# A transformer block on one core: the second MLP weight prepared earlier in parts that share tiles with the transposed rows, sums copied out by ScalarE, rows of x loaded earlier, the norm split by groups

## The chip, the cores and the metric

One Trainium2 chip, one of its NeuronCores. The metric is the device time of the whole program in microseconds (us), the median over runs. Besides, one execution was recorded by the hardware profiler; its span is the time from the first to the last recorded instruction. TensorE (PE) multiplies, VectorE (DVE), ScalarE (ACT) and GpSimd (POOL) work element by element, SyncE (SP) issues nearly all DMA transfers, in one queue.

## The reference

```python
mod = (_silu(c) @ w_mod).reshape(c.shape[0], 6, 1, -1)
sa, ca, ga, sb, cb, gb = (mod[:, i] for i in range(6))
h = _layernorm(x, axis=-1) * (1 + ca) + sa
x = x + ga * _A_ref(h, A_wq, A_wk, A_wv, A_wo)      # 32 query heads of 16, one key/value head
h = _layernorm(x, axis=-1) * (1 + cb) + sb
x = x + gb * _B_ref(h, B_w1, B_b1, B_w2, B_b2)      # gelu(h @ w1 + b1) @ w2 + b2, tanh form
```

x has 2048 rows of 512, all in float32; w1 is 512 x 1376, w2 1376 x 512. A product of full precision is made of three products of rounded parts, high and low: names in H and L are these pairs (`w2H`, `w2L`, `gH`, `gL`, `onH`, `onL`).

## The kernel before

**Blocks, units, steps, cycles.** The 2048 rows are worked off in 8 blocks of 256. Attention of a block is 8 units (`u`, four heads each), a unit is 8 steps over the keys. Two steps make one turn of the main loop, a cycle; `clock[0]` rises by 4 in it. In a cycle TensorE makes 8 products `m` (scores whose row maxima VectorE takes ahead, line 523), 8 products `e` (scores for the exponentials that ScalarE makes, line 599) and at the end of each step 16 products `acc` (line 610, probabilities by values).

**The rest of a block rides along.** Everything after attention, the output product (`wops`), the second layer norm, the transposes (`tp`), the two MLP products (`w1ps`, `w2ps`), is a generator, `rest_steps`, and so are the query projections (`qps`) of later rows. Each cycle takes one batch of products from the first generator that is ready. A batch of more than 4.8 in units of 512 columns (12 products of 256 columns are 6.0) is mixed in as two halves of the rows of the systolic array with one pattern, a lighter one (`LIGHT`) with another pattern that opens with an exponential's product, a cycle without a batch with a third. `W2_PARTS` cuts the 33 products of each of a block's four second MLP sums (two tiles of rows, t, by two halves of the columns) into batches. The fourth sum is put between the next block's `wops` and its transposes (`second`).

**Banks.** Batches' sums lie in one PSUM bank, "x"; it must be read out before the next sum begins. The exponentials' products use three banks in turn. So the element-wise operation that reads a finished sum is waited for by the next sum's first product. `store` does this for the second MLP: VectorE adds the sum to the rows of x (`x1`, tile "x1", two buffers) into `ot`, and SP sends `ot` two clock ticks later.

**Work put off.** `later(n, fn)` runs `fn` n clock ticks on, that is, puts its instructions into the engines' orders there. No scheduler moves anything: the order in which the code runs is the order of each engine, and engines wait for each other by semaphores only. So an engine may run ahead, but SP and GpSimd take their own instructions strictly one after the other.

**From attention to the output product.** When a block's attention ends, `rest` lets SP load the sums (`rsum`), VectorE invert them, SP write them to `drs`, and `fetch_half` load per group g of 128 columns the heads (`os`, from `do`) and the inverted sums (`os`, from `drs`), groups 0 and 1 first, 2 and 3 four ticks later. `norm` then lets GpSimd multiply the four groups and split all of them at once into `onH` and `onL`. `fetch_rest` loads x (512 KB) when the block's output product begins, and three tiles of w1.

**Weights.** Between the attention products GpSimd prepares w1, then wo, then w2, one tile of 128 rows each four ticks (`PREP`): SP loads it (`w2f`, three buffers; the last tile has 96 rows, and GpSimd clears it first), GpSimd multiplies by the gate and splits it. `w2H` and `w2L` are one tile each for all 11 row tiles and take the place of `bigH`, `bigL`, the transposed rows of blocks 1 to 3 (of 512 rows each) that the query projections read. So w2 starts only when the last projection has been sent (`state["q"] == 0`).

**Loads that TensorE must not meet late.** `load_q` loads a unit's queries into `qst`, in six DMAs, two cycles ahead of their first use. `heed` notes each DMA with a tick, and `wait_early` makes an `acc` product that comes after this tick wait for it:

```python
heed(nc.sync.dma_start(out=raw(qst[64 * s:64 * s + 16]), in_=low), n)       # n = 6 if s else 8
...
if kt % 2 or cidx:
    wait_early(ins)                                                          # one DMA per acc product
```

Of the kernel before, what the change touches and what calls it, by code (L numbers as in the profile page):

```python
# [34 lines left out]
LIGHT = 4.8  # L35
Q_LIGHT = 12
Q_SIZES = ((6, 6), (4, 4, 4))
W2_PARTS = ((12, 12, 9), (9, 8, 8, 8), (9, 8, 8, 8), (12, 12, 9))
TAIL = (4, 8)
GROUP = 4  # L40
NORM_WAIT = 8
# [11 lines left out]
def adaln_mqa_mlp(  # L53
# [15 lines left out]
    nc = tc.nc  # L69
    _, S, D = x.shape  # L70
# [3 lines left out]
    KD = D // P  # L74
    BQ = 512
    NB = S // BQ
# [4 lines left out]
    NF = (F + P - 1) // P  # L81
# [4 lines left out]
    blocks = [(r, HQ) for r in range(0, S, HQ)]  # L86

    xf = x[0]
# [3 lines left out]
    att = ctx.enter_context(tc.tile_pool(name="att", bufs=1))  # L92
# [37 lines left out]
    def split(dst_h, dst_l, src, eng_h, eng_l, between=None):  # L130
        if eng_h is nc.gpsimd:
            eng_h.tensor_scalar(out=dst_h, in0=src, scalar1=1.0, scalar2=0.0, op0=ALU.mult, op1=ALU.add)
        elif eng_h is nc.scalar:
            eng_h.copy(dst_h, src)
        else:
            eng_h.tensor_copy(out=dst_h, in_=src)
        if between:
            between()
        eng_l.tensor_tensor(out=dst_l, in0=src, in1=raw(dst_h), op=ALU.subtract)  # L139
# [3 lines left out]
    state = {"mods": False, "q": NB * KD}  # L143
# [193 lines left out]
    hts = {}  # L337
    hts_stats = {}
    pad(att, 64, "pad5")
    bigH = att.tile([P, NB - 1, KD, BQ], F32R, name="bigH", tag="bigH")  # L340
    bigL = att.tile([P, NB - 1, KD, BQ], F32R, name="bigL", tag="bigL")
    hts[0] = (att.tile([P, KD, BQ], F32R, name="h0H", tag="opk"), att.tile([P, KD, BQ], F32R, name="h0L", tag="woH"))
    for b in range(1, NB):
        hts[b] = (bigH[:, b - 1], bigL[:, b - 1])

    pad(att, 64, "pad6")
    tps = {}
# [348 lines left out]
    def rest(b, fast):  # L696

        rp = wts_pool["rest"]
        row0, w = blocks[b]
        spread = ["m", "e", "m", "e", "m", "e", "v"] if fast else ["x"]  # L700
        turn = [0]

        def bank():
            turn[0] += 1
            tag = spread[turn[0] % len(spread)]
            return ebank() if tag == "e" else dict(tag=tag, bufs=3 if tag == "m" else 1)

        oss, ons = {}, {}

        def fetch():  # L710

            n = H * w // P
            rsum = att.tile([P, n], F32, name=f"rsum{b}", tag="rsum", bufs=1)
            nc.sync.dma_start(out=rsum, in_=do[b][:, :, 16, :].rearrange("q c (t n) -> (q c) t n", n=n))

            def invert():
                nc.vector.reciprocal(out=rsum, in_=rsum)
                later(1, scatter)

            def scatter():  # L720
                nc.sync.dma_start(out=drs[b].rearrange("h (t n) -> (h t) n", n=n), in_=rsum)
                fetch_half(0)

            later(4, invert)

        def fetch_half(hf):
            os_ = att.tile([P, 2, KD, HQ], F32, name=f"os{b}_{hf}", tag="opk", bufs=1)
            cols = slice(hf * HQ, (hf + 1) * HQ)

            def fetch_heads(gs):  # L730
                for g in gs:
                    src = do[b][2 * g:2 * g + 2, :, 0:16, cols].rearrange("q c r n -> (q c) r n")
                    nc.sync.dma_start(out=os_[:, 0, g, :], in_=src)
                    src = drs[b][8 * g:8 * g + 8, cols].unsqueeze(1).to_broadcast([8, 16, HQ])
                    nc.sync.dma_start(out=os_[:, 1, g, :], in_=src)


            fetch_heads(range(KD // 2))
            later(4, lambda: fetch_heads(range(KD // 2, KD)))
            oss[hf] = os_  # L740
            later(7, lambda: norm(hf))

        def norm(hf):
            if fast:
                g = KD - 1
                split(state["on"][0][:, g, :], state["on"][1][:, g, :], state["os"][:, 0, g, :], nc.scalar, nc.vector)
                return
            onH = att.tile([P, KD, HQ], F32R, name=f"onH{b}_{hf}", tag="xH", bufs=2)
            onL = att.tile([P, KD, HQ], F32R, name=f"onL{b}_{hf}", tag="xL", bufs=2)
            ons[hf] = (onH, onL)  # L750
            os_ = oss.pop(hf)
            for g in range(KD):
                nc.gpsimd.tensor_tensor(out=os_[:, 0, g, :], in0=os_[:, 0, g, :], in1=os_[:, 1, g, :], op=ALU.mult)  # L753
            split(onH, onL, os_[:, 0], nc.gpsimd, nc.gpsimd)
            if (hf + 1) * HQ < w:
                later(6, lambda: fetch_half(hf + 1))
            ready[hf] = clock[0] + NORM_WAIT

        ready = {}
        later(*((4, lambda: norm(0)) if fast else (2, fetch)))  # L760
        return rest_steps(b, fast, rp, bank, ons, ready)

    early = {}

    def fetch_w1(b, w1ts, f):
        w1ts[f] = wts_pool["rest"].tile([P, 2, KD, P], F32R, name=f"w1t{b}_{f}", tag="w1t", bufs=3)
        heed(nc.sync.dma_start(out=raw(w1ts[f]), in_=dw1[f]), 8 if f > 2 else 24)

    def fetch_rest(b):

        row0, w = blocks[b]
        x1 = wts_pool["rest"].tile([P, 2, D], F32, name=f"x1_{b}", tag="x1", bufs=2)
        nc.sync.dma_start(out=x1, in_=xf[row0:row0 + w, :].rearrange("(t p) d -> p t d", p=P))
        w1ts = {}
        for f in range(3):
            if b == len(blocks) - 1:
                fetch_w1(b, w1ts, f)
            else:
                later(W1_TURNS * (f + 1), lambda f=f: fetch_w1(b, w1ts, f))
        early[b] = x1, w1ts  # L780
# [8 lines left out]
    def rest_steps(b, fast, rp, bank, ons, ready):  # L789
# [6 lines left out]
        for hf in range(w // HQ):  # L796
# [188 lines left out]
            def store(t, ps, cols=slice(0, D)):  # L985
                row = row0 + hf * HQ + t * P
                ot = rp.tile([P, D], F32, name=f"ot{b}_{hf}_{t}_{cols.start}", tag="ot", bufs=2)
                nc.vector.tensor_tensor(out=ot[:, cols], in0=ps[:, :cols.stop - cols.start], in1=x1[:, t, cols], op=ALU.add)  # L988
                send = lambda: nc.sync.dma_start(out=of[row:row + P, cols], in_=ot[:, cols])
                if fast:  # L990
                    send()
                else:
                    later(2, send)
# [4 lines left out]
            def second_sum(t, cols, size):  # L998
                n = cols.stop - cols.start
                sl = slice(t * P, (t + 1) * P)  # L1000
                place = dict(tag="m", bufs=3) if b == len(blocks) - 2 and t else bank()
                ps = psum.tile([P, n], F32, name=f"w2ps{b}_{hf}_{t}_{cols.start}", **place)
                ops = [(gH[:, f, sl], gL[:, f, sl], w2H[:, f, cols], w2L[:, f, cols]) for f in range(NF)]
                yield from batches(ps, ops, size, lambda f: made.issuperset(range(f + 1)))
                if fast:
                    later(1, lambda t=t, ps=ps, cols=cols: store(t, ps, cols))
                    yield 2
                else:
                    store(t, ps, cols)
# [12 lines left out]
    def put_by(b):  # L1022

        return b < len(blocks) - 2
# [90 lines left out]
    def prep_w2():  # L1115
        rp = wts_pool["rest"]
        wfs = {}

        def load(f):
            fw = min(P, F - f * P)  # L1120
            wf = wfs[f] = rp.tile([P, D], F32, name=f"w2f{f}", tag="wf", bufs=3)
            if fw < P:
                nc.gpsimd.memset(wf, 0.0)
            nc.sync.dma_start(out=wf[:fw], in_=w2[f * P:f * P + fw, :])

        def work(f):
            nc.gpsimd.tensor_tensor(out=wfs[f], in0=wfs[f], in1=gb, op=ALU.mult)
            split(w2H[:, f, :], w2L[:, f, :], wfs[f], nc.gpsimd, nc.gpsimd)

        return prepare(NF, load, work)  # L1130

    weights = ["w1", "wo", "w2"]
    preps = {}
# [171 lines left out]
    while mp.done < lead[0]:  # L1305
        chunk(1)
    preps["w1"] = prep_w1()
    w2H = w2L = None
    prepared = [0]

    def issue(*groups):
# [28 lines left out]
    for u in range(NU):  # L1340
        for K in range(0, steps[u], 2):
# [76 lines left out]
            end_step(u, X)  # L1418
            behind = (u, Y)
            clock[0] += 1  # L1420
            if state["mods"] and state["q"] == 0 and w2H is None:
                w2H = att.tile([P, NF, D], F32R, name="w2H", tag="bigH")
                w2L = att.tile([P, NF, D], F32R, name="w2L", tag="bigL")
                preps["w2"] = prep_w2()
            if clock[0] >= prepared[0] + PREP and weights and weights[0] in preps:
                prepared[0] = clock[0]
# [53 lines left out]
```

## Time and profile before

| | us |
|---|---|
| median of 3 runs (1595.82 to 1596.21) | 1595.88 |
| the profiled execution, its own time | 1594.15 |
| its span | 1592.4 |
| TensorE busy in it | 1558.2 |
| VectorE, ScalarE, GpSimd busy in it | 1413.8, 1199.7, 665.5 |

The page's rows name an instruction by engine, source line, operation and tiles, written tile first. TensorE is busy nearly all the time, so the reading turns on the few places where it is not, and on how long each step takes. In a timeline a row is start, length, engine, line, operation, tiles and how many equal instructions were merged; in brackets stands the idle time of the engine before it and what ended it. Times count from the span's start.

### The profile page before, as it was taken

To read this page: it belongs to the slowest core of one execution; us is meant where nothing else is said; L and a number is where in the kernel's file an instruction comes from. 1 tells how busy PE (TensorE), PEld (TensorE's weight loads), DVE (VectorE), ACT (ScalarE), POOL (GpSimd) and SP (SyncE) were. 2 spreads that over 40 slices of the span, in tenths; PEclk is the share of its full clock that TensorE was granted. 3 is DMA by queue.
4 is the path that set the end of the run, shared out by engine and by line. 5 is a ranking of instruction groups with operands and counts; after the bars stand their busy time and mean duration, and the time that the engine had idled before them with its cause. 6 is when DMAs were issued, how large, how long until landed. Compare 5 with 4: busy or idle time off the path is not lost.

```text
span 1592.4 us, 43322 instructions
## 1 busy us (share of the span) xinstructions
PE 1558.2 (98%) x17491; PEld 1044.7 (66%) x17491; DVE 1413.8 (89%) x2515; ACT 1199.7 (75%) x2393; POOL 665.5 (42%) x1176
## 2 busy tenths in 40 slices
PE   6999999899999999999999999999999999999999
PEld 3466655557666676666767676666766676666767
DVE  7899999799999999999999999999999999999715
ACT  5577777678877887778877887778877788778853
POOL 4445431686503372235612364224712364224721
PEclk8999999999999999999999999999999999999999
DMA  8136311413112120212112130212112130121231
GB/s 264 70 112 204 113 55 58 129 40 108 33 53 69 47 95 22 89 35 90 51 37 87 44 99 19 64 59 83 57 35 88 35 109 19 48 82 52 96 135 72
DMA packets 81022, 121.74 MB, mean 76 GB/s; under 512 B 15966, under 2 KB 55646, under 8 KB 80564
## 3 DMA queue, kind: packets, MB, share of 16 engines
q1 hardware_dynamic: 80804, 118.95, 22.9%
q8 instruction: 137, 2.24, 0.6%
q14 instruction: 65, 0.53, 0.1%
q10 hardware_dynamic: 16, 0.00, 0.0%
HBM read 91.13 MB, written 27.27 MB: 74 GB/s over the span
## 4 chain that ended last, share of the span: by engine, by line
PE 86%; DVE 6%; POOL 3%; DMA 2%; SPq 1%; issue 1%; ACT 0%; DVEq 0%; POOLq 0%; ACTq 0%
PE acc L610 29%; PE e L598 17%; PE m L518 17%; PE w1ps L193 8%; PE w2ps L193 6%; DVE mx L523 5%; PE wops L193 3%; PE qps L193 2%; PE w2ps L187 2%; PE w1ps L187 1%; DMA xt<-in_A_x_dram 1%; PE tp L193 1%; PE kps L164 1%; DMA os<-drs 1%; DMA x<-in_A_x_dram 0%
## 5 line engine op out<-in xcount | busy, mean ns | idle before, releaser
L523 DVE TENSOR_REDUCE mx<-m 128x1 f32<-128x512 f32 x2048 | 1272.6, 680 | 97.4 <-PE m L518 83.6
L599 ACT ACTIVATE p<-e 128x512 f32<-128x512 f32 x2048 | 1065.5, 601 | 307.5 <-PE e L598 212.4
L518 PE MATMUL m<-ks,qst 64*128 64x512 f32 x2048 | 829.7, 434 | 7.2 <-DMA qst<-dq 4.0
L598 PE MATMUL e<-qst,ks 64*128 64x512 f32 x2048 | 737.5, 412 | 1.4 <-ACT wqH L334 1.3
L610 PE MATMUL acc<-p,va 128*32 128x256 f32 x8192 | 549.6, 386 | 0.0
L598 PEld LDWEIGHTS e<-qst,ks 64*128 64x128 f32 x2048 | 361.1, 185 | 113.4 <-ACT p L599 103.9
L518 PEld LDWEIGHTS m<-ks,qst 64*128 64x128 f32 x2048 | 367.8, 184 | 101.9 <-DVE mx L523 81.7
L610 PEld LDWEIGHTS acc<-p,va 128*32 128x32 f32 x8192 | 214.1, 109 | 215.1 <-issue 111.8
L193 PE MATMUL w1ps<-h2H,w1t 64*128 64x256 f32 x1232 | 236.2, 288 | 0.0
L567 POOL TENSOR_SCALAR mt<-turned 8x32 f32<-8x32 f32 x256 | 53.1, 208 | 404.3 <-DVE turned L573 392.3
L193 PEld LDWEIGHTS w1ps<-h2H,w1t 64*128 64x128 f32 x1232 | 184.0, 185 | 31.7 <-issue 22.2
L193 PE MATMUL w1ps<-h2L,w1t 64*128 64x256 f32 x616 | 169.4, 275 | 0.3 <-POOL h2L L139 0.3
L193 PE MATMUL w2ps<-w2H,gH 64*128 64x256 f32 (+1 forms) x546 | 159.0, 291 | 1.2 <-DVE ot L988 1.2
L193 PE MATMUL w2ps<-w2L,gH 64*128 64x256 f32 (+1 forms) x546 | 153.4, 281 | 0.0
L193 PE MATMUL w2ps<-w2H,gL 64*128 64x256 f32 (+1 forms) x546 | 153.4, 281 | 0.0
L193 PEld LDWEIGHTS w1ps<-h2L,w1t 64*128 64x128 f32 x616 | 113.5, 184 | 0.5 <-POOL h2L L139 0.5
L193 PEld LDWEIGHTS w2ps<-w2H,gH 64*128 64x128 f32 x546 | 100.7, 184 | 9.7 <-issue 5.4
L193 PEld LDWEIGHTS w2ps<-w2H,gL 64*128 64x128 f32 x546 | 100.7, 184 | 2.6
L193 PEld LDWEIGHTS w2ps<-w2L,gH 64*128 64x128 f32 x546 | 100.6, 184 | 1.3
L941 POOL TENSOR_SCALAR tt<-tt 128x256 f32<-128x256 f32 x77 | 31.0, 403 | 137.5 <-ACT tt L940 137.5
L193 PE MATMUL wops<-woH,onH 64*128 64x256 f32 x224 | 68.3, 305 | 6.6 <-DVE x L811 6.0
L753 POOL TENSOR_TENSOR os<-os 128x256 f32<-128x256 f32 x28 | 20.6, 734 | 111.5 <-DMA os<-drs 111.5
(188 smaller groups left out, 1623.6 us busy)
## 6 DMA issues: line engine op xcount, KB each, us to landing
w1t<-dw SPq DMA_DIRECT2D x82, 512.0 KB
qst<-dq SPq DMA_DIRECT2D x128, 64.0 KB
do<-oc SPq DMA_DIRECT2D x64, 128.0 KB
dw<-w1s SPq DMA_DIRECT2D x11, 512.0 KB
xt<-in_A_x_dram SPq DMA_DIRECT2D x4, 1024.0 KB
dq<-qH SPq DMA_DIRECT2D x16, 256.0 KB
dq<-qL SPq DMA_DIRECT2D x16, 256.0 KB
qst<-dq SPq DMA_DIRECT2D x128, 32.0 KB
```

What stands on the lines that cost most here:

```text
L164: nc.tensor.matmul(ps, a, b_, start=begin and n == 0, stop=end and n == last)
L187: nc.tensor.matmul(ps, a, b_, start=first_, stop=last_)
L193: nc.tensor.matmul(ps, a[rows], b_[rows], start=first_ and s == 0, stop=last_ and s == 1)
L518: nc.tensor.matmul(m, qsts[u][rows, j, t * P:(t + 1) * P], ks[rows, kc * 512:(kc + 1) * 512], start=True, stop=True)
L523: nc.vector.tensor_reduce(out=self.mx[u][:, i, kc:kc + 1], in_=m, axis=AX.X, op=ALU.max)
L567: nc.gpsimd.tensor_scalar(out=mt[:, g:g + 32], in0=turned[g:g + 4 * T, :], scalar1=1.0, scalar2=0.0, op0=ALU.mult, op1=ALU.add)
L598: nc.tensor.matmul(e, ks[rows, kt * P:(kt + 1) * P], rhs, start=True, stop=True)
L599: nc.scalar.activation(ptiles[u, K][:, j, s, :], e, AF.Exp, scale=0.25)
L610: ins = nc.tensor.matmul(accs[u][32 * cidx:32 * cidx + 32, :], va[:, kt, :], rhs, start=kt == 0, stop=kt == NKT - 1)
L753: nc.gpsimd.tensor_tensor(out=os_[:, 0, g, :], in0=os_[:, 0, g, :], in1=os_[:, 1, g, :], op=ALU.mult)
L941: nc.gpsimd.tensor_scalar(out=tt, in0=tt, scalar1=1.0, scalar2=1.0, op0=ALU.mult, op1=ALU.add)
```

## The change

**Second weight.** `bigH` and `bigL` become six tiles, one pair for each of blocks 1 to 3 (`big1H` and so on). `w2s` holds three pairs of weight tiles of four row tiles each (the last has three), which take the places of these pairs one after the other. `prep_w2` starts when wo is done, ten cycles sooner, and goes on to a pair only when the projections from its rows have been sent. **Copies.** For blocks 0 to 5 `store` lets ScalarE copy the sum to `ot`; GpSimd adds x a tick later, SP sends four ticks later. **Parts.** The second and third sums of a block are cut (12, 8, 8, 5) instead of (9, 8, 8, 8). **Rows of x.** `fetch_x` is called with the second half of the `os` loads, a cycle sooner. **Norm.** Each group is split right after its multiplication.

```diff
-W2_PARTS = ((12, 12, 9), (9, 8, 8, 8), (9, 8, 8, 8), (12, 12, 9))
+W2_PARTS = ((12, 12, 9), (12, 8, 8, 5), (12, 8, 8, 5), (12, 12, 9))
...
-    bigH = att.tile([P, NB - 1, KD, BQ], F32R, name="bigH", tag="bigH")
-    bigL = att.tile([P, NB - 1, KD, BQ], F32R, name="bigL", tag="bigL")
+    bigs = [[att.tile([P, KD, BQ], F32R, name=f"big{b}{p_}", tag=f"big{b}{p_}") for b in range(1, NB)] for p_ in "HL"]
...
             later(4, lambda: fetch_heads(range(KD // 2, KD)))
+            later(4, lambda: fetch_x(b))
...
                 nc.gpsimd.tensor_tensor(out=os_[:, 0, g, :], in0=os_[:, 0, g, :], in1=os_[:, 1, g, :], op=ALU.mult)
-            split(onH, onL, os_[:, 0], nc.gpsimd, nc.gpsimd)
+                split(onH[:, g, :], onL[:, g, :], os_[:, 0, g, :], nc.gpsimd, nc.gpsimd)
...
+    def fetch_x(b):
+        row0, w = blocks[b]
+        x_rows[b] = wts_pool["rest"].tile([P, 2, D], F32, name=f"x1_{b}", tag="x1", bufs=2)
+        nc.sync.dma_start(out=x_rows[b], in_=xf[row0:row0 + w, :].rearrange("(t p) d -> p t d", p=P))
...
-                nc.vector.tensor_tensor(out=ot[:, cols], in0=ps[:, :cols.stop - cols.start], in1=x1[:, t, cols], op=ALU.add)
+                part = ps[:, :cols.stop - cols.start]
                 send = lambda: nc.sync.dma_start(out=of[row:row + P, cols], in_=ot[:, cols])
+                if put_by(b):
+                    nc.scalar.copy(ot[:, cols], part)
+                    later(1, lambda: nc.gpsimd.tensor_tensor(out=ot[:, cols], in0=ot[:, cols], in1=x1[:, t, cols], op=ALU.add))
+                    later(4, send)
+                    return
+                nc.vector.tensor_tensor(out=ot[:, cols], in0=part, in1=x1[:, t, cols], op=ALU.add)
...
         def work(f):
+            g = f // KD
+            if f % KD == 0:
+                w2s.append([att.tile([P, min(KD, NF - f), D], F32R, name=f"w2{p_}{g}", tag=f"big{g + 1}{p_}") for p_ in "HL"])
             nc.gpsimd.tensor_tensor(out=wfs[f], in0=wfs[f], in1=gb, op=ALU.mult)
-            split(w2H[:, f, :], w2L[:, f, :], wfs[f], nc.gpsimd, nc.gpsimd)
-        return prepare(NF, load, work)
+            split(w2s[g][0][:, f % KD, :], w2s[g][1][:, f % KD, :], wfs[f], nc.gpsimd, nc.gpsimd)
+        for i, _ in enumerate(prepare(NF, load, work)):
+            yield
+            while i >= 1 and i - 1 < NF and not sent.issuperset(((i - 1) // KD + 1, g) for g in range(KD)):
+                yield
...
-            if state["mods"] and state["q"] == 0 and w2H is None:
-                w2H = att.tile([P, NF, D], F32R, name="w2H", tag="bigH")
-                w2L = att.tile([P, NF, D], F32R, name="w2L", tag="bigL")
+            if state["mods"] and "w2" not in preps:
                 preps["w2"] = prep_w2()
```

How this moves instructions is seen at three places. First SP's queue in block 0, at the second pair of `os` loads (`w2f` are loads of the second weight, `x1_0` the rows of x, `do1` the next block's attention sums). Before:

```order
L1124 DMA w2f1_3971<-in_B_w2_dram 128x512
L733 DMA os0_0_3894<-do0_114 128x1x256
L735 DMA os0_0_3894<-drs0_106 128x1x256
L733 DMA os0_0_3894<-do0_114 128x1x256
L735 DMA os0_0_3894<-drs0_106 128x1x256
L1124 DMA w2f2_4054<-in_B_w2_dram 128x512
L623 DMA do1_115<-oc8_4089 128x256
L1124 DMA w2f3_4133<-in_B_w2_dram 128x512
L1124 DMA w2f4_4213<-in_B_w2_dram 128x512
L773 DMA x1_0_4215<-in_A_x_dram 128x2x512
```

And after:

```order
L732 DMA os0_0_3950<-do0_114 128x1x256
L734 DMA os0_0_3950<-drs0_106 128x1x256
L732 DMA os0_0_3950<-do0_114 128x1x256
L734 DMA os0_0_3950<-drs0_106 128x1x256
L773 DMA x1_0_4034<-in_A_x_dram 128x2x512
L622 DMA do1_115<-oc8_4152 128x256
```

The weight's loads are gone from here, and the rows of x follow the `os` loads. Second, some ten DMAs earlier in the same queue and at that place in GpSimd's order (`ml9` is the last part of a unit's maxima). SP's queue after, from the last weight tile on (before, the first weight tile `w2f0`, without a clearing, stands ahead of the same `drs`):

```order
L1138 DMA w2f10_3946<-in_B_w2_dram 96x512
L720 DMA drs0_106<-rsum0_3845 128x64
L732 DMA os0_0_3950<-do0_114 128x1x256
L734 DMA os0_0_3950<-drs0_106 128x1x256
L732 DMA os0_0_3950<-do0_114 128x1x256
L734 DMA os0_0_3950<-drs0_106 128x1x256
L487 DMA qst3_161<-dq_0_1_88 16x2x256
```

GpSimd before:

```order
L132 TENSOR_SCALAR qH3_3_3782<-q32_3_3_3780 128x512
L139 TENSOR_TENSOR qL3_3_3783<-q32_3_3_3780,qH3_3_3782 128x512
L567 TENSOR_SCALAR mt9_3793<-turned9_3792 8x32 x4
L132 TENSOR_SCALAR mh9_3794<-mt9_3793 8x128
L139 TENSOR_TENSOR ml9_3795<-mt9_3793,mh9_3794 8x128
L753 TENSOR_TENSOR os0_0_3894<-os0_0_3894 128x256 x4
L132 TENSOR_SCALAR onH0_0_4035<-os0_0_3894 128x1024
L139 TENSOR_TENSOR onL0_0_4036<-os0_0_3894,onH0_0_4035 128x1024
```

And after:

```order
L139 TENSOR_TENSOR ml9_3842<-mt9_3840,mh9_3841 8x128
L1144 TENSOR_TENSOR w2f7_3683<-w2f7_3683,gb_83 128x512
L132 TENSOR_SCALAR w2H1_3591<-w2f7_3683 128x512
L139 TENSOR_TENSOR w2L1_3592<-w2f7_3683,w2H1_3591 128x512
L1144 TENSOR_TENSOR w2f8_3762<-w2f8_3762,gb_83 128x512
L132 TENSOR_SCALAR w2H2_3941<-w2f8_3762 128x512
L139 TENSOR_TENSOR w2L2_3942<-w2f8_3762,w2H2_3941 128x512
L1137 MEMSET w2f10_3946 128x512
L1144 TENSOR_TENSOR w2f9_3865<-w2f9_3865,gb_83 128x512
L132 TENSOR_SCALAR w2H2_3941<-w2f9_3865 128x512
L139 TENSOR_TENSOR w2L2_3942<-w2f9_3865,w2H2_3941 128x512
```

Weight tiles 7 to 9 and the clearing of tile 10 now stand between a unit's maxima and the norm of the first block, and the load of tile 10 stands ahead of `drs` in SP's queue. Third, the end of block 1's fourth sum. VectorE before:

```order
L523 TENSOR_REDUCE mx28_10913<-m28_1_1_2_0_11276 128x1
L523 TENSOR_REDUCE mx28_10913<-m28_1_1_3_0_11286 128x1
L988 TENSOR_TENSOR ot1_0_1_256_11293<-w2ps1_0_1_256_10998,x1_1_7392 128x256
L523 TENSOR_REDUCE mx29_11315<-m29_0_0_0_1_11316 128x1
L523 TENSOR_REDUCE mx29_11315<-m29_0_0_1_1_11324 128x1
```

ScalarE after:

```order
L598 ACTIVATE p27_1_11291<-e27_1_0_1_11292 128x512
L598 ACTIVATE p27_1_11291<-e27_1_0_0_11299 128x512
L598 ACTIVATE p27_1_11291<-e27_1_1_0_11314 128x512
L999 COPY ot1_0_1_256_11326<-w2ps1_0_1_256_11031 128x256
L598 ACTIVATE p27_1_11291<-e27_1_1_1_11331 128x512
L598 ACTIVATE p27_2_11344<-e27_2_0_0_11345 128x512
```

The sum leaves its bank ahead of the step's fourth exponential, and not after the step's last maximum.

More of the change, by code (lines that the diff above doesn't have):

```diff
@@ L339, in adaln_mqa_mlp @@
     pad(att, 64, "pad5")
-    bigH = att.tile([P, NB - 1, KD, BQ], F32R, name="bigH", tag="bigH")
-    bigL = att.tile([P, NB - 1, KD, BQ], F32R, name="bigL", tag="bigL")
+    bigs = [[att.tile([P, KD, BQ], F32R, name=f"big{b}{p_}", tag=f"big{b}{p_}") for b in range(1, NB)] for p_ in "HL"]
     hts[0] = (att.tile([P, KD, BQ], F32R, name="h0H", tag="opk"), att.tile([P, KD, BQ], F32R, name="h0L", tag="woH"))
     for b in range(1, NB):
-        hts[b] = (bigH[:, b - 1], bigL[:, b - 1])
+        hts[b] = (bigs[0][b - 1], bigs[1][b - 1])
     pad(att, 64, "pad6")
@@ L767, in fetch_w1 @@
         heed(nc.sync.dma_start(out=raw(w1ts[f]), in_=dw1[f]), 8 if f > 2 else 24)
+    def fetch_x(b):
+        row0, w = blocks[b]
+        x_rows[b] = wts_pool["rest"].tile([P, 2, D], F32, name=f"x1_{b}", tag="x1", bufs=2)
+        nc.sync.dma_start(out=x_rows[b], in_=xf[row0:row0 + w, :].rearrange("(t p) d -> p t d", p=P))
+    x_rows = {}
     def fetch_rest(b):
-        row0, w = blocks[b]
-        x1 = wts_pool["rest"].tile([P, 2, D], F32, name=f"x1_{b}", tag="x1", bufs=2)
-        nc.sync.dma_start(out=x1, in_=xf[row0:row0 + w, :].rearrange("(t p) d -> p t d", p=P))
+        if b not in x_rows:
+            fetch_x(b)
+        x1 = x_rows.pop(b)
         w1ts = {}
@@ L1002, in second_sum @@
                 ps = psum.tile([P, n], F32, name=f"w2ps{b}_{hf}_{t}_{cols.start}", **place)
-                ops = [(gH[:, f, sl], gL[:, f, sl], w2H[:, f, cols], w2L[:, f, cols]) for f in range(NF)]
+                ops = [(gH[:, f, sl], gL[:, f, sl], *w2_pair(f, cols)) for f in range(NF)]
                 yield from batches(ps, ops, size, lambda f: made.issuperset(range(f + 1)))
@@ L1126, in work, with w2_pair @@
         def work(f):
+            g = f // KD
+            if f % KD == 0:
+                w2s.append([att.tile([P, min(KD, NF - f), D], F32R, name=f"w2{p_}{g}", tag=f"big{g + 1}{p_}") for p_ in "HL"])
             nc.gpsimd.tensor_tensor(out=wfs[f], in0=wfs[f], in1=gb, op=ALU.mult)
-            split(w2H[:, f, :], w2L[:, f, :], wfs[f], nc.gpsimd, nc.gpsimd)
-        return prepare(NF, load, work)
+            split(w2s[g][0][:, f % KD, :], w2s[g][1][:, f % KD, :], wfs[f], nc.gpsimd, nc.gpsimd)
[3 more added lines that the diff above has]
+                yield
+    w2s = []
+    def w2_pair(f, cols):
+        return [t[:, f % KD, cols] for t in w2s[f // KD]]
     weights = ["w1", "wo", "w2"]
@@ L1307, in adaln_mqa_mlp @@
     preps["w1"] = prep_w1()
-    w2H = w2L = None
     prepared = [0]
```

## The prediction

> **What bounds the kernel now.** I read the page's chain first, then the TensorE timeline through the span, then the waits at the steps that stick out.
>
> ```profile
> PE 1558.2 (98%) x17491; PEld 1044.7 (66%) x17491; DVE 1413.8 (89%) x2515; ACT 1199.7 (75%) x2393; POOL 665.5 (42%) x1176
> PE 86%; DVE 6%; POOL 3%; DMA 2%; SPq 1%; issue 1%; ACT 0%; DVEq 0%; POOLq 0%; ACTq 0%
> ```
>
> TensorE's order sets the end almost everywhere, so a change pays only where TensorE stands still or where a step is longer than its kind. The timeline of TensorE's `acc` groups shows this best: sixteen `acc` products close each step, and two steps make one cycle. From one group's start to the next is the length of a step.
>
> ```profile
> 604.14 1.07 PE L610 MATMUL acc<-p,va 128*32 128x256 f32 x16
> 607.04 1.07 PE L610 MATMUL acc<-p,va 128*32 128x256 f32 x16
> 609.88 1.07 PE L610 MATMUL acc<-p,va 128*32 128x256 f32 x16
> ...
> 618.25 1.07 PE L610 MATMUL acc<-p,va 128*32 128x256 f32 x16
> 621.44 1.07 PE L610 MATMUL acc<-p,va 128*32 128x256 f32 x16
> 624.17 1.07 PE L610 MATMUL acc<-p,va 128*32 128x256 f32 x16
> ```
>
> The first three rows are a cycle with a full batch of 12 products: steps of 2.90 and 2.84, 5.74 us together. The last three are a cycle with a light batch (9 products) right after a sum was copied out by VectorE: 3.19 and 2.73. A light step is thus 2.73, and the store costs its cycle 0.46. Now the steps that stick out:
>
> ```profile
> 290.29 1.07 PE L610 MATMUL acc<-p,va 128*32 128x256 f32 x16
> 294.13 1.07 PE L610 MATMUL acc<-p,va 128*32 128x256 f32 x16
> 296.97 1.07 PE L610 MATMUL acc<-p,va 128*32 128x256 f32 x16
> ...
> 310.63 1.07 PE L610 MATMUL acc<-p,va 128*32 128x256 f32 x16
> ...
> 343.87 1.07 PE L610 MATMUL acc<-p,va 128*32 128x256 f32 x16
> 347.71 1.07 PE L610 MATMUL acc<-p,va 128*32 128x256 f32 x16
> 350.32 1.07 PE L610 MATMUL acc<-p,va 128*32 128x256 f32 x16
> 353.84 1.07 PE L610 MATMUL acc<-p,va 128*32 128x256 f32 x16
> ...
> 480.31 1.07 PE L610 MATMUL acc<-p,va 128*32 128x256 f32 x16
> 484.45 1.07 PE L610 MATMUL acc<-p,va 128*32 128x256 f32 x16
> ...
> 1396.20 1.07 PE L610 MATMUL acc<-p,va 128*32 128x256 f32 x16
> 1399.82 1.07 PE L610 MATMUL acc<-p,va 128*32 128x256 f32 x16
> ```
>
> All but the last two pairs lie in the first block's output product and MLP, where GpSimd also prepares the second MLP's weight. The largest one, 296.97 to 310.63, is a wait for the rows of x:
>
> ```profile
> 303.23 0.42 DVE L811 TENSOR_TENSOR x<-wops,x 128x256 f32<-128x256 f32 x1 [6.28 <-DMA x<-in_A_x_dram]
> 303.71 0.58 PE L193 MATMUL wops<-woH,onH 64*128 64x256 f32 x1 [5.66 <-DVE x L811]
> ```
>
> **The change, part by part.** *Rows of x sooner, weight sooner.* The load of x stood in SP's queue behind weight loads that waited for GpSimd buffers; now it follows the last four `os` loads, a cycle earlier, and no weight load stands between. Then 296.97 to 310.63 (13.66) becomes one full cycle (5.74): 7.92 gained, of which 5.66 is the idle time and 2.26 the slow clock after it (below). The same edit takes the wait at 1396.20 (3.62 against 2.84): 0.78. With GpSimd free of the weight, 343.87 to 347.71 (3.84 against a light step's 2.73) gives 1.11 and 350.32 to 353.84 (3.52 against 2.84) 0.68.
>
> *Norm by groups.* GpSimd split all four groups at once, after the last had come:
>
> ```profile
> 271.68 0.43 SPq L1124 DMA_DIRECT2D w2f<-in_B_w_dram  x1
> 272.21 2.52 DMA drs<-rsum
> 278.82 0.46 SPq L491
> 283.50 4.40 DMA os<-drs
> 288.03 0.73 POOL os L753
> 289.98 2.38 POOL onL L139
> ```
>
> These are the chain's rows up to the first `wops` product (with SP's own row ahead), and 290.29 to 294.13 (3.84 against 2.90) is the wait for `onL`: 0.94. Splitting each group as it lands takes most of `onL`'s 2.38 off the end. The same wait in the second block, 480.31 to 484.45 (4.14 against 2.90), goes with the store there: 1.24. Splitting in four costs GpSimd more instructions, but it sits idle between the groups' landings.
>
> *ScalarE copies the sums out.* 24 VectorE additions become 24 ScalarE copies and 24 GpSimd additions. A copy of this size from PSUM is in the trace, and so is the place where one will stand:
>
> ```profile
> 701.60 0.37 ACT L620 COPY oc<-acc 128x256 f32<-128x256 f32 x1 [0.28 <-PE acc L610]
> 701.99 2.06 ACT L599 ACTIVATE p<-e 128x512 f32<-128x512 f32 x4
> ...
> 703.21 1.07 PE L610 MATMUL acc<-p,va 128*32 128x256 f32 x16
> 706.35 1.07 PE L610 MATMUL acc<-p,va 128*32 128x256 f32 x16
> ```
>
> The copy goes ahead of the fourth exponential, whose end moves from 704.05 to 704.42. TensorE's next step opened at 704.21 (the VectorE store kept it to 706.35, 3.14). If its first product needs that exponential's bank, as in the light cycle of the transposes, it opens about 0.29 late (0.08 from end to start is an estimate from gaps between dependent rows): 2.73 + 0.29 = 3.02, and 0.12 is gained, six times, 0.7. Where the next cycle opens with a full batch, its products and a maximum stand ahead of that exponential and hide it: 5.92 (618.25 to 624.17) becomes 5.74, 0.18 gained, three times in five blocks, 2.7. That is what the parts (12, 8, 8, 5) buy: a full cycle costs 0.28 more than a light one (5.74 against 2 x 2.73), paid out of the store's 0.46. In the first block the third sum's price eats the first's gain: 0. Together 3.4; bounds: 24 x 0.46 = 11.0 and, if every copy delays TensorE by 0.29 more, -1.8. I take 3.4, from the row of the full cycle. GpSimd's additions (0.73, the `os` row) and SP's sends behind them lie cycles ahead of the buffers' next use; if GpSimd were late, SP's query loads behind the send would be late next. Separate tiles for the transposed rows add no instruction.
>
> *What the earlier weight takes the place of.* GpSimd works it off among the last query splits:
>
> ```profile
> 269.03 0.45 POOL L139 TENSOR_TENSOR ml<-mt,mh 8x128 fp32r<-8x128 f32 x1
> 292.30 1.30 POOL L1127 TENSOR_TENSOR w2f<-w2f,gb 128x512 f32<-128x512 f32 x1
> 295.64 1.29 POOL L1127 TENSOR_TENSOR w2f<-w2f,gb 128x512 f32<-128x512 f32 x1
> 341.43 0.54 POOL L1123 MEMSET w2f<- 128x512 f32 x1
> 282.47 1.07 PE L610 MATMUL acc<-p,va 128*32 128x256 f32 x16
> ```
>
> One row tile of the weight takes 3.34 (292.30 to 295.64). After `ml` (to 269.48) there now stand two of them and the clearing of the last, short tile: 269.48 + 6.68 + 0.54 = 276.70. Before it SP may not issue that tile's load, and behind this load in SP's queue are `drs`, four `os` loads and six query loads. `drs` goes at 276.70 + 0.53 = 277.2, 5.0 later than 272.21; the third query load (SPq L491) at 283.8 instead of 278.82. It lands about 2.5 later (the nearest row, `drs`; at most 4.40, the `os` row), at 286.3, and the `acc` group of 282.47 is tied to it by `wait_early`. TensorE stands still for 3.8 us, where before it did not. The `os` loads, also late, are then covered by this stall. Does the clock fall?
>
> ```profile
> 76.50:79.90 3.40, 2.38 (x11) 1.42 (x12) 2.43 (x5) 3.26 (x8) 3.05 (x5) 1.00 0.29 77
> 80.00:83.30 3.30, 3.30 (x23) 1.43 (x20) 3.30 (x6) 2.16 (x5) 0.00 (x0) 0.50 0.43 130
> 345.40:348.80 3.40, 2.48 (x24) 1.17 (x24) 1.94 (x4) 3.00 (x6) 3.23 (x4) 1.00 0.01 2
> ```
>
> In this table by stretch the first number after the length is TensorE's busy time, the last but two the granted clock. 2.38 busy of 3.40 was followed by half clock, 2.48 was not. A stall of 3.8 leaves at most 1.5 busy, so I take the fall, at 2.26 as after the wait for x: 6.1 in all (bounds 0 and 8.0).
>
> The Trainium skill says otherwise: "TensorE: Matmul & The Clock Gate", Part 1 (the HAM clock gate), lets the clock drop after at least one idle window of about 3.4 us, and windows run free, so 3.8 us would seldom hold a whole one; by it the sum would be 2.26 us better. The stretch at 76.50 fell with TensorE busy for 70% of it, against the page, so the row decides.
>
> Sum: 7.92 + 0.78 + 1.11 + 0.68 + 0.94 + 1.24 + 3.4 - 6.1 = 10.0. The profiled execution took 1594.15 (span 1592.4): it would take 1584.2. It lies 1.73 under the median of the runs, 1595.88, which becomes 1585.9.
>
> **The rivals.** (1) No new stall: SP's chain is shorter than I think, or the query loads land in time. For it: before, the third load had 3.6 us to spare (278.82 to 282.47); against it, GpSimd's order. 1595.88 - 16.1 = 1579.8. (2) The stall, but full clock, the page's rule as a mechanism: 1583.6. (3) Each ScalarE copy holds TensorE up by 0.29 in the 18 other places too, because a bank is needed sooner than I read: +5.2, 1591.1. For it: the fourth exponential ends only 0.16 before the next step opens. (4) Slower: GpSimd falls behind during the earlier row tiles as well, and SP's weight loads then hold the query loads of two more units. It decides from the point where a load is 4.4 us late in both places, each then 4.4 + 2.26 = 6.7: +13.4, 1599.3. Against it: by the rows GpSimd has 3.34 to do per cycle of 5.5 plus a split now and then. (5) No change: the load of x, now behind late `os` loads, is late all the same and the 7.92 stays: 1593.8.
>
> **How the numbers follow.** Forecast 0.43, (1) 0.23, (2) 0.18, (3) 0.08, (4) 0.04, (5) 0.04. About 0.2% (3.2 us) is what a measurement of this kernel can tell from no change. Faster by more: 0.43 + 0.23 + 0.18 + 0.08 = 0.92; within: 0.04; slower: 0.04. The range runs from under (1), with the light cycles' stores fully gained, to short of (3): 1579.0 to 1590.0; outside are (4), (5), (3) and the tails.
>
> **What would show it.** Right: no wait of VectorE for x; full cycles of 5.74 where sums are copied out; `acc` groups near 282.5 and the next one some 6 us apart and half clock just after; `drs` near 277. Wrong: that gap missing, or `acc` steps over 3.0 wherever ScalarE copies a sum, or new waits for query loads between 215 and 265 us.

## The result and the profile after

The changed kernel takes 1585.78 us (median of 4 runs, 1583.89 to 1589.15) against 1596.05 for the kernel before beside it: a ratio of 0.9935, 95% interval 0.9916 to 0.9954. The execution that was profiled is the slowest of the four: 1589.15, span 1587.3. The page's busy times, and the shares of its chain:

```profile
PE 1562.7 (98%) x17491; PEld 1043.9 (66%) x17491; DVE 1406.0 (89%) x2491; ACT 1204.3 (76%) x2417; POOL 692.8 (44%) x1242
PE 94%; ACT 3%; DVE 1%; DMA 1%; issue 0%; SPq 0%; POOL 0%; DVEq 0%; ACTq 0%
```

GpSimd and VectorE hardly hold the chain any more (before 3% and 6%), yet TensorE is busy for longer. The profiled span fell by only 5.1 us, because the start took 5 us longer, in part at half clock. Two stretches there, of before first and of after second (busy times of PE, PEld, DVE, ACT, POOL, then granted clock, DMA share, GB/s):

```profile
47.74:51.15 3.41, 3.41 (x20) 2.39 (x19) 3.41 (x7) 2.99 (x5) 3.33 (x5) 1.00 0.61 247
```

```profile
47.74:51.15 3.41, 3.41 (x14) 1.95 (x12) 2.47 (x5) 2.69 (x6) 3.14 (x4) 0.50 0.85 293
```

So I measure the main loop by itself, from the first of the 512 `acc` groups to the 511th (start of the group's last product). It took 1455.68 us before and 1445.26 after: 10.4 less, as the medians say (10.3). TensorE's `acc` groups of after, around the two places of block 0:

```profile
282.31 1.07 PE L609 MATMUL acc<-p,va 128*32 128x256 f32 x16
284.92 1.07 PE L609 MATMUL acc<-p,va 128*32 128x256 f32 x16
287.53 0.62 PE L609 MATMUL acc<-p,va 128*32 128x256 f32 x2
289.00 0.62 PE L609 MATMUL acc<-p,va 128*32 128x256 f32 x2 [0.85 <-DMA qst<-dq]
290.44 1.24 PE L609 MATMUL acc<-p,va 128*32 128x256 f32 x12 [0.82 <-DMA qst<-dq]
293.21 1.07 PE L609 MATMUL acc<-p,va 128*32 128x256 f32 x16
...
298.45 1.07 PE L609 MATMUL acc<-p,va 128*32 128x256 f32 x16
301.33 1.07 PE L609 MATMUL acc<-p,va 128*32 128x256 f32 x16
304.19 1.07 PE L609 MATMUL acc<-p,va 128*32 128x256 f32 x16
...
310.18 1.07 PE L609 MATMUL acc<-p,va 128*32 128x256 f32 x16
```

The new stall is there: a group that should be done 1.07 us after 287.53 is cut in three, waits twice for query loads, and its cycle takes 8.29 instead of 5.22. Where before waited 5.66 us for x, the cycle 304.19 to 310.18 takes 5.99. The first `wops` step, 298.45 to 301.33, is 2.88. GpSimd's and SP's rows ahead of the stall, and the chain's row of the load that ended it:

```profile
281.13 0.54 POOL L1137 MEMSET w2f<- 128x512 f32 x1
281.69 0.34 SPq L1138 DMA_DIRECT2D w2f<-in_B_w_dram  x1
282.12 0.38 SPq L720 DMA_DIRECT2D drs<-rsum  x1
286.23 0.61 SPq L487 DMA_DIRECT2D qst<-dq  x1
286.89 0.68 SPq L488 DMA_DIRECT2D qst<-dq  x1
286.89 3.51 DMA qst<-dq
```

This execution runs 5.06 us behind that of before here (the `acc` group of 282.47 starts at 287.53). Without that the clearing ends at 276.6 and `drs` goes at 277.1, where the prediction had 276.70 and 277.2.

Kernels and runs, with the place of the first `acc` group (start of its last product) and the main loop of the profiled execution. Each ratio is to runs of the kernel before made beside it, whose medians were 1596.05 to 1596.84:

| kernel | median us (n) | ratio to before, 95% | first group | main loop |
|---|---|---|---|---|
| before | 1595.88 (3) | | 83.02 | 1455.68 |
| after | 1585.78 (4) | 0.9935 (0.9916 to 0.9954) | 88.19 | 1445.26 |
| after, again | 1585.85 (5) | 0.9936 (0.9923 to 0.9950) | 84.44 | 1445.43 |
| 1 last tile put off | 1581.49 (4) | 0.9909 (0.9895 to 0.9923) | 83.59 | 1441.72 |
| 2 VectorE copies out | 1593.94 (11) | 0.9980 (0.9971 to 0.9989) | 84.65 | 1452.23 |
| 3 old parts | 1584.81 (5) | 0.9924 (0.9911 to 0.9936) | 86.79 | 1442.32 |
| 4a stall 2.2 longer | 1591.22 (1) | | 86.44 | 1449.34 |
| 4b stall 4.3 longer | 1596.84 (1) | | 88.44 | 1452.95 |
| 5 before, x sooner only | 1592.62 (12) | 0.9979 (0.9968 to 0.9989) | 84.06 | 1449.94 |
| 6 last tile put off, old parts | 1578.47 (4) | 0.9888 (0.9874 to 0.9902) | 85.50 | 1439.04 |
| 7 weight late | 1585.52 (5) | 0.9937 (0.9924 to 0.9949) | 84.60 | 1446.30 |
| 8 as 6, norm whole | 1587.49 (5) | 0.9952 (0.9938 to 0.9965) | 84.30 | 1445.38 |

### The profile page after: what moved, and what is told of

The parts are those of the page before. It is cut to its first block, busy times and chain, and to the rows that moved or that the text cites. A ratio compares the mean times of both kernels' runs of the same rounds, so it can differ in the third digit from the quotient of the medians.

```text
span 1587.3 us, 43409 instructions
## 1 busy us (share of the span) xinstructions
PE 1562.7 (98%) x17491; PEld 1043.9 (66%) x17491; DVE 1406.0 (89%) x2491; ACT 1204.3 (76%) x2417; POOL 692.8 (44%) x1242
## 4 chain that ended last, share of the span: by engine, by line
PE 94%; ACT 3%; DVE 1%; DMA 1%; issue 0%; SPq 0%; POOL 0%; DVEq 0%; ACTq 0%
PE acc L609 32%; PE e L597 19%; PE m L517 19%; PE w1ps L193 8%; PE w2ps L193 6%; PE wops L193 3%; PE qps L193 2%; ACT p L598 2%; PE w2ps L187 2%; PE w1ps L187 1%; DVE mx L522 1%; PE tp L193 1%; PE kps L164 1%; PE tp L371 0%; PE modr L289 0%; DMA wm<-in_w_mod_dram 0%
## 5 line engine op out<-in xcount | busy, mean ns | idle before, releaser
L597 PE MATMUL e<-qst,ks 64*128 64x512 f32 x2048 | 729.5, 411 | 2.0 <-ACT wqH L334 1.3
L597 PEld LDWEIGHTS e<-qst,ks 64*128 64x128 f32 x2048 | 356.9, 184 | 112.6 <-ACT p L598 102.6
L193 PE MATMUL wops<-woL,onH 64*128 64x256 f32 x224 | 62.2, 278 | 0.0
```

What stands on the lines that cost most here:

```text
L193: nc.tensor.matmul(ps, a[rows], b_[rows], start=first_ and s == 0, stop=last_ and s == 1)
L597: nc.tensor.matmul(e, ks[rows, kt * P:(kt + 1) * P], rhs, start=True, stop=True)
```

## The experiments

**After, again.**

> The changed kernel, unchanged. In its first profiled execution the main loop began 5.0 us later than before (the first cycles end at 93.98 instead of 88.91), with the granted clock at half from 47.7 to 57 us, where it was full before. Theory: the start is left to chance by the clock, the main loop gains 10.5 us in every execution; then the median is again 1585 to 1586.5, and single runs differ by the start alone. Rival: the change itself makes the start 5 us longer; then the first cycle ends near 94 in this profile too, and a start without it would give 1580.8.

The median is the same, the main loop too, and the first group came at 84.44 instead of 88.19. Over all kernels it lies between 83.0 and 88.4. The slow start of the first profile was chance. Rival refuted.

**1. The stall taken away.** The generator of the second weight pauses three cycles before its last tile, so that the load of this tile stands behind the query loads in SP's queue.

```diff
             while i >= 1 and i - 1 < NF and not sent.issuperset(((i - 1) // KD + 1, g) for g in range(KD)):
                 yield
+            if i == NF - 2:
+                for _ in range(3):
+                    yield
```

> The load and the clearing of the second weight's last tile are put off by three cycles, so that SP's queue has the inverted sums (drs), the os loads and the query loads ahead of it. Theory: the cycle of 8.29 us (acc waiting for qst<-dq, 1.7 idle) becomes a plain one of 5.2, all else stays: 3.1 less than after, 1582.7. Rival 1: the next late thing takes its place (the norm, or os loads, at the first wops product: 5.74 becomes up to 6.7, as before): 1583.7. Rival 2: the two row tiles of the weight that are now worked off behind the norm hold up the next unit's maxima and queries: a new stall of up to 3.3, 1586.

The `acc` groups at the place, which keep their 2.6:

```profile
280.28 1.07 PE L609 MATMUL acc<-p,va 128*32 128x256 f32 x16
282.90 1.07 PE L609 MATMUL acc<-p,va 128*32 128x256 f32 x16
285.50 1.07 PE L609 MATMUL acc<-p,va 128*32 128x256 f32 x16
```

The cycle takes 5.22 instead of 8.67 (after, again), the main loop 3.71 less; neither rival's new wait appears. The clearing and loading of one short tile ahead of `drs` cost all of the stall.

**2. VectorE copies out, new parts.** The `put_by(b)` branch of `store` is removed.

> After, with the sums copied out by VectorE as before (parts 12, 8, 8, 5 kept). Theory A: the 5.70 us of a cycle that ends a sum with five products (5.51 with eight before) come from the five products, not from ScalarE's copy: it stays 5.70, and the 23 cycles that follow a store lengthen by 0.13 to 0.24, some 3.9 in all: 1589.7. Theory B: the 5.70 come from the copy, which stands ahead of the third exponential there: those twelve cycles fall back to 5.52 (-2.1), the others lengthen by 3.9: 1587.6.

TensorE's groups at the end of block 1's second sum (five products), and the longest wait after its first sum:

```profile
614.66 0.39 PE L193 MATMUL w2ps<-w2H,gH 64*128 64x256 f32 x1 [0.62 <-DVE ot L998]
...
630.35 1.07 PE L609 MATMUL acc<-p,va 128*32 128x256 f32 x16
633.20 1.07 PE L609 MATMUL acc<-p,va 128*32 128x256 f32 x16
636.05 1.07 PE L609 MATMUL acc<-p,va 128*32 128x256 f32 x16
```

The cycle with five products has two steps of 2.85 here, where no copy stands on ScalarE. Theory A holds on that: the five products cost it. The total came out higher than either theory: the main loop grew by 6.8, not 3.9, because the full cycle that now follows the first sum takes 6.42 to 6.70 (before, with a light batch there, 5.89 to 5.94), with TensorE waiting 0.62 for VectorE's store, six times. The new parts are bad with VectorE's copies.

**3. ScalarE copies out, old parts.**

```diff
-W2_PARTS = ((12, 12, 9), (12, 8, 8, 5), (12, 8, 8, 5), (12, 12, 9))
+W2_PARTS = ((12, 12, 9), (9, 8, 8, 8), (9, 8, 8, 8), (12, 12, 9))
```

> After, with the old parts (9, 8, 8, 8) and ScalarE's copies. By sum, after: 5.74 + 5.49 + 5.49 + 5.70 = 22.42 us. Theory A (the five products cost, the copy delays the next light cycle by 0.29, the prediction's reading): 5.49 + 0.29 + 5.49 + 5.49 + 5.52 = 22.28, 12 sums: 1.7 less than after, 1584.1. Theory B (a copy costs 0.18 in any light cycle that ends a sum, and 0.29 in the next): 22.46, no difference: 1586.3. Theory C (a copy in a light cycle is hidden): 22.0, 5.0 less: 1580.8.

The groups at the end of block 1's second sum: first of this kernel, then of after.

```profile
630.49 1.07 PE L609 MATMUL acc<-p,va 128*32 128x256 f32 x16
633.23 1.07 PE L609 MATMUL acc<-p,va 128*32 128x256 f32 x16
636.00 1.07 PE L609 MATMUL acc<-p,va 128*32 128x256 f32 x16
638.90 1.07 PE L609 MATMUL acc<-p,va 128*32 128x256 f32 x16
641.65 1.07 PE L609 MATMUL acc<-p,va 128*32 128x256 f32 x16
```

```profile
631.92 1.07 PE L609 MATMUL acc<-p,va 128*32 128x256 f32 x16
634.77 1.07 PE L609 MATMUL acc<-p,va 128*32 128x256 f32 x16
637.62 1.07 PE L609 MATMUL acc<-p,va 128*32 128x256 f32 x16
640.47 1.07 PE L609 MATMUL acc<-p,va 128*32 128x256 f32 x16
643.35 1.07 PE L609 MATMUL acc<-p,va 128*32 128x256 f32 x16
```

In each fence the first two steps are the cycle that ends the sum, with the copy in the second, and the last two are the next sum's first cycle. Old parts: 2.74 + 2.77, then 2.90 + 2.75. New parts: 2.85 + 2.85, then 2.85 + 2.88. A copy by ScalarE delays the next light step by some 0.16 (2.90 against 2.73 to 2.75), not 0.29, and a light start after it takes 5.65, less than a full one (5.73). The main loop is 3.1 us shorter than with the new parts, near the middle between theory A (1.7) and theory C (5.0); B is refuted. The medians alone (1584.81 and 1585.85, single runs of 1582.8 to 1586.8 and 1585.2 to 1588.7) would not have told it, the cycles do: 0.16 to 0.23 less in eleven of the twelve that end a sum with five products, 0.07 to 0.11 less in eleven of the twelve that now open light after a copy.

**4. The stall made longer.** The last tile is cleared five and nine times instead of once.

```diff
-                nc.gpsimd.memset(wf, 0.0)
+                for _ in range(5):      # 4b: 9
+                    nc.gpsimd.memset(wf, 0.0)
```

> After, with the last weight tile cleared five times instead of once (0.54 us each on GpSimd), so that SP's queue is held 2.16 us longer. The cycle of 8.67 us (2.0 idle, granted clock 1.00 throughout) should become 10.8 with some 4.2 us idle, about the stall of 3.8 that the prediction had. Theory A (the prediction's row: a stretch of 3.4 us with TensorE busy for 2.4 or less is followed by half clock): half clock for one stretch behind the stall, the cycles after it 2.3 us longer in sum. Theory B (only a stretch with TensorE idle throughout is): the clock stays 1.00 here, unless the stretch lies wholly within the idle time.

> The same with nine clearings: 4.3 us longer than in after, a cycle of about 13 us with some 6.4 idle, more than the 5.66 after which the kernel before showed half clock. Both theories A (a stretch that is busy for less than 2.4 of 3.4) and B (an idle stretch) have half clock behind it for 3.4 us, the following cycles 1.7 to 2.3 us longer in sum.

The stretches on the clock's own steps of 3.41 us: after, then 4a, then 4b.

```profile
286.32:289.73 3.41, 2.45 (x12) 0.81 (x8) 2.72 (x5) 2.06 (x4) 2.37 (x4) 1.00 0.36 116
289.73:293.14 3.41, 2.69 (x20) 1.41 (x20) 0.77 (x2) 1.37 (x4) 1.31 (x3) 1.00 0.31 89
293.14:296.55 3.41, 3.41 (x41) 1.76 (x40) 3.27 (x6) 2.86 (x7) 1.54 (x3) 1.00 0.67 202
```

```profile
286.88:290.29 3.41, 0.00 (x0) 0.00 (x0) 0.69 (x2) 0.04 (x1) 2.15 (x4) 1.00 0.39 114
290.29:293.70 3.41, 2.90 (x14) 1.27 (x14) 0.00 (x0) 0.00 (x0) 1.50 (x3) 0.50 0.31 99
293.70:297.11 3.41, 3.41 (x32) 1.82 (x30) 2.48 (x4) 2.57 (x6) 1.39 (x3) 1.00 0.80 217
```

```profile
286.66:290.07 3.41, 1.84 (x10) 0.68 (x6) 2.73 (x5) 2.06 (x4) 3.11 (x3) 1.00 0.35 105
290.07:293.49 3.42, 0.00 (x0) 0.00 (x0) 0.00 (x0) 0.00 (x0) 1.13 (x2) 0.50 0.38 123
293.49:296.90 3.41, 1.87 (x10) 0.90 (x12) 0.00 (x0) 0.00 (x0) 2.53 (x4) 0.50 0.16 48
296.90:300.31 3.41, 3.41 (x18) 1.79 (x10) 0.94 (x2) 1.74 (x4) 0.31 (x1) 0.50 0.55 170
300.31:303.72 3.41, 3.41 (x41) 1.68 (x40) 3.19 (x6) 2.58 (x6) 3.01 (x6) 1.00 0.52 181
```

In after TensorE was busy for 2.45 and 2.69 in the two stretches that hold the stall, and no half clock followed. In 4a a stretch was idle throughout, and one of half clock followed: the cycle takes 12.12, 1.3 more than the added 2.16 explain. In 4b half clock began behind a stretch that was busy for 1.84 and lasted three stretches, and the cycle takes 15.04, 2.05 more than the added 4.32. Both kernels ran once, and both are compared with after, again (8.67). Theory B does not explain 4b's first stretch. Theory A's threshold of about 2.4 does not hold either: in experiment 3, which has the stall too, less busy time was followed by full clock.

```profile
287.14:290.56 3.42, 1.69 (x14) 0.72 (x14) 0.71 (x2) 0.06 (x1) 2.55 (x5) 1.00 0.22 58
290.56:293.97 3.41, 3.41 (x31) 1.86 (x31) 2.48 (x4) 2.61 (x6) 0.53 (x1) 1.00 0.62 153
```

**5. Kernel before, with the rows of x sooner only.** `fetch_x` is called behind the second half of the `os` loads, as in after.

```diff
             later(4, lambda: fetch_heads(range(KD // 2, KD)))
+            later(4, lambda: fetch_x(b))
```

> The kernel before with one edit: the rows of x are loaded behind the os loads, as in after. Theory: the wait of 5.66 us with its slow clock goes, and the one in block 6: 7.7 to 7.9 + 0.75, so the main loop (first to last cycle's end) shrinks by 8.5 us and the median to 1588. Rival 1: only the idle time goes and another wait (the second half of os, the weight that GpSimd prepares at this time) holds the next products: 5 to 6, 1590.5. Rival 2: the load of x, 512 KB, keeps the weight's loads back, and GpSimd's lateness moves into the MLP's cycles: 1 to 2 us less of gain.

The long cycle fell from 13.66 to 6.73, block 6's wait went too (0.73), and the first `wops` cycle of block 0 fell by 0.60, to 6.08. But the cycle after the long one grew by 0.97, and first `wops` cycles of four later blocks by 0.17 to 0.59: the main loop gained 5.7, the size of rival 1, and not 8.5. The lower gain of the median (3.65) has the chance of the start in it: single runs go from 1589.6 to 1596.5.

**6. The two better halves together.** Last tile put off as in 1, old parts as in 3.

> After, with the last weight tile put off by three cycles and the old parts (9, 8, 8, 8). Theory: the two gains are in different cycles and add up: the main loop shrinks by 3.5 to 3.7 (no stall) and 3.1 (12 sums x 0.27) against after: 1585.8 - 6.7 = 1579.1. Rival: with shorter cycles GpSimd's additions and the sends come late at one place, and 1 to 2 us are given back: 1580.5.

1578.47 and a main loop 6.4 shorter than after's: the gains add up but for a little, and this version beats both kernels. The rival is there on a small scale: one cycle, near 645 us, takes 6.16 instead of 5.48, with TensorE waiting for a query load.

**7. The weight late again.** All else as in after.

```diff
-            if state["mods"] and "w2" not in preps:
+            if state["mods"] and state["q"] == 0 and "w2" not in preps:
```

> After, with the second weight started late again, when the last projection has been sent (the shared tiles, copies, parts, rows of x and norm as in after). Theory: the early weight alone brings two things, the stall of the query loads (+3.07 and +3.45 in two executions) and the MLP's first cycles without a wait for GpSimd (-1.15 and -0.68); without it the main loop changes by -3.3 + 1.8 = -1.5 us against after: 1584.3. Rival: with GpSimd busy on the weight during the norm and the query splits, the first wops products wait again (+0.9, up to +2 with x landing late): no gain or up to 1 us more than after, 1586.8.

TensorE's wait for query loads at `acc` products, out of the waits view (us in total, times, longest):

```profile
PE acc L609 <- DMA qst<-dq: 0.2, 1, 0.2
```

The stall of 1.7 to 2.0 is gone (-3.45 in its cycle), but 1.16 and 0.66 come back in the MLP's first cycles, and 0.95 is lost in the cycle after the x place, as in 5. The main loop differs by 0.9 from after's, the median by 0.3: the rival's side. In after, the ten cycles of earlier weight were worth almost nothing, since their stall took back what they brought. With the last tile put off (1), they are worth 4.6 (1446.30 against 1441.72).

**8. The norm whole, on top of 6.**

```diff
-                split(onH[:, g, :], onL[:, g, :], os_[:, 0, g, :], nc.gpsimd, nc.gpsimd)
+            split(onH, onL, os_[:, 0], nc.gpsimd, nc.gpsimd)
```

> The version without the stall and with the old parts (1578.5), with the norm undone: GpSimd splits the four groups at once after the last one. Theory: the first wops product of each block waits for onL again: +0.94 in block 0 and some 1.0 in block 1, as before, and 0.2 to 0.6 in blocks 2 to 6, where the early load of x made those cycles longer when it was added alone: +2 to +4 in all, 1580.5 to 1582.5. Rival: without the weight behind it GpSimd is in time and the split of four groups at once is hidden: 1578.5.

TensorE's waits for the norm (waits view), and the row of the longest, in block 1:

```profile
PE wops L193 <- POOL onL L139: 3.2, 4, 1.1
473.98 0.38 PE L193 MATMUL wops<-woH,onL 64*128 64x256 f32 x1 [1.08 <-POOL onL L139]
```

The first `wops` cycles of blocks 1 to 6 grow by 1.65, 1.55, 0.55, 0.69, 1.40 and 0.84: 6.7, more than theory's upper end. That of block 0 does not change at all. The profiled execution is the fastest of the five; its main loop is 6.3 longer than that of 6, the median 9.0 higher, and the runs spread over 5.9 us.

## Why the prediction was right, and where it was not

The time forecast, 1585.9, was met by 0.1 us, but not by its own sum: stall and clock together cost 3 us less than forecast, copies and parts brought 1.3 less, and 1.0 more was lost where nothing was forecast. That these nearly cancel is luck, and to 0.1 us the more so, as single runs of one kernel differ by 5 and more. Term by term, as predicted and as measured in after by cycles:

| term | predicted | measured |
|---|---|---|
| wait for x, block 0 | 7.92 | 7.67 |
| wait for x, block 6 | 0.78 | 0.75 |
| MLP's first cycles | 1.11 + 0.68 | 1.16 + 0.67 |
| first `wops` step | 0.94 | 0.94 |
| second block's `wops` | 1.24 | 1.26 |
| copies and parts | 3.4 | 2.1 |
| new stall | -3.8 | -3.07 (-3.45 again) |
| slow clock behind it | -2.26 | 0 |

The measured terms make 11.5. The main loop gained 10.4: the other 1.0 went to cycles elsewhere, three of them longer by 0.14 to 0.28.

**The stall** came where and for the reason forecast, link by link: the weight's tiles, the clearing, SP held, `drs` 4.9 later than before. Its end was placed 1.0 us too late (286.3, measured 290.40 less 5.06): TensorE's last wait was for the second query load, not the third, though that one took 3.51 to land instead of 2.5.

**The clock** is the step that failed. "A stall of 3.8 leaves at most 1.5 busy" was wrong: the group ran on in pieces, TensorE was idle for only 1.67 in its two waits (0.85 + 0.82), and it was busy for 2.45 and 2.69 of the two stretches that hold the stall. The prediction's row of 345.40 could not mark a safe value either, since it lies across two of the clock's steps: one ends at 346.19, and in it TensorE was busy for 2.60. Nor does the row of 76.50 hold for this place, where 1.69 did no harm in experiment 3. The mechanism was that of rival (2), stall without slow clock. The Trainium skill's rule ("TensorE: Matmul & The Clock Gate", Part 1: the clock drops after an idle window of about 3.4 us) gave the right result here against the prediction, and 4a agrees with it: one idle stretch, then half clock. So does the wait for x in the kernel before, idle from 298.40 to 301.81, with half clock behind it. 4b does not (1.84 busy, then half clock), nor did 76.50. Rival (2)'s time, 1583.6, was missed by 2.2, mainly because of the next point and the 1.0 above.

**Copies and parts.** The cycles that open full after a copy went down by 0.13 to 0.24, as read (0.18), save one in block 0 (+0.21) and the first `wops` cycle of block 4 (-0.51, from 6.22), and the six at the transposes by 0.20 to 0.23 rather than 0.12, because a copy costs the next light step some 0.16 and not the 0.29 derived from the fourth exponential. What the sum left out is the batch of five products: it was priced like any light cycle, with no row to show one, and takes 5.70 instead of 5.51. Twelve of them cost some 2.0 us. "That is what the parts buy" was wrong twice over: the parts lose 3.1 (3) where ScalarE copies, and with the old parts the same cycles bring some 5, where the change as made brought 2.1. The trace shows where the 0.19 arises, half in each of the two steps. A row of TensorE's weight loads in after, in the step that opens at 631.92:

```profile
634.10 0.19 PEld L597 LDWEIGHTS e<-qst,ks 64*128 64x128 f32 x2 [0.30 <-ACT p L598]
```

With five products the last two `e` start together, 2.18 us into the step, after a wait of 0.30 for an exponential, and the last `m` starts at 2.53. With eight (3) the third `e` starts at 2.03 without a wait, and the last `m` at 2.31 to 2.35. The wait stands in all 20 such steps of blocks 1 to 5 in after and in all 20 in experiment 2; an order of the five products without it was not tried.

**The norm.** The 0.94 of block 0 was put down to the split by groups alone. But that cycle takes 5.72 with the whole norm and the early weight (8), and 5.72 with the split and the late weight (7); with neither, x alone brings it to 6.08 (5). So the split is not needed for it where the weight is early. The 1.24 of the second block stands (1.65 in 8). What the prediction did not see is how much the split is worth once the rest is changed: the whole norm costs 6.7 in blocks 1 to 6 (8), so "norm by groups" is a large part of the change, and its rows in the kernel before could not show that. Why it costs so much there is only in part known. The early load of x alone lengthens the same cycles by 1.2 in sum (5). In block 2 `onL` ends 0.64 us after the last product of the `acc` group ahead of `wops` has started in the kernel before, 0.81 after with x alone, 1.98 after in 8; what makes the last step was not separated.

**Rivals.** (1) is what 1 makes of the kernel: 1581.5, against 1579.8 estimated. The 3.6 us that spoke for it ran from a load's issue, not from its landing: in the kernel before the second query load was issued at 278.09, and if it took 3.51 as in after, it landed at 281.60 (an estimate), 0.9 ahead of the group. (3), a copy's cost in every place, is refuted by 3; (4) and (5) did not occur.

## What to carry to other kernels

When an early preparation is moved ahead, follow the one queue it shares with urgent loads to the last item: here one clearing of 0.54 us behind 6.7 us of row tiles, with the load that waits for it ahead of the urgent ones, cost 3.5 us, and moving that one load brought it all back. Price every batch size that a new split creates from a row that has this size: fewer products were slower. A forecast that meets the time can still hold two wrong terms, so compare the terms cycle by cycle, and keep the start of the program, which varies by 5 us from run to run, out of it.

## What was unexpected of the hardware

Half clock came in steps of 3.41 us, and TensorE's busy time in the step before does not tell whether it comes. Near 80 us TensorE waits some 1.35 for an exponential's first product in every kernel. Two such steps, of after and of 4a, and the step that followed each:

```profile
81.52:84.93 3.41, 2.24 (x11) 1.29 (x11) 2.45 (x5) 3.26 (x9) 3.05 (x5) 1.00 0.29 62
84.93:88.34 3.41, 3.41 (x23) 1.76 (x23) 3.41 (x6) 2.41 (x5) 0.00 (x0) 0.50 0.54 149
```

```profile
78.66:82.08 3.42, 2.08 (x18) 0.72 (x14) 2.90 (x5) 1.80 (x6) 1.20 (x2) 1.00 0.06 16
82.08:85.49 3.41, 3.31 (x16) 1.84 (x15) 2.71 (x5) 3.19 (x8) 1.86 (x4) 1.00 0.59 173
```

With 11 products in the step half clock followed, with 18 it did not, though the busy time was less. At the stall 10 products were followed by half clock (4b) and 14 by full (3). But at the start of after a step with 18 products and 2.84 us of busy time (43.97 to 47.39) was followed by half clock, and these 11 in after, again, by full:

```profile
282.31:285.72 3.41, 2.25 (x11) 1.00 (x11) 2.93 (x5) 2.06 (x4) 2.02 (x4) 1.00 0.35 122
285.72:289.14 3.42, 2.54 (x21) 1.20 (x19) 0.19 (x1) 0.80 (x2) 1.66 (x3) 1.00 0.34 100
```

What decides stays open.
